# Row-tiled remainder matmuls, scores copied out as bf16, and rescaling on GpSimd in a fused attention forward and backward

## The chip, the core and the metric

The kernel runs on one core of one Trainium2 chip. The core has a matrix engine (TensorE, PE in the profile, with its weight loads as PEld), a vector engine (VectorE, DVE), an activation engine (ScalarE, ACT), a general engine (GpSimd, POOL), a queue that only issues DMAs (SyncE, SP), and 16 DMA engines. Matrix results land in PSUM; everything else lives in SBUF. The metric is the device time of one execution in microseconds (us), as the median of several runs.

## What is computed

The reference is one branchformer block and its backward pass, for x of shape 2 x 4000 x 144 in bf16. A layer norm feeds an attention branch and a gated convolution branch; both are merged by a depthwise convolution and a projection. What matters here is the attention:

```python
xa = _layernorm(x, axis=-1)
qkv = jnp.einsum('btd,de->bte', xa, w_qkv)
q, k, v = ...
scores = jnp.einsum('btd,bsd->bts', q, k) * D ** (-0.5)
p = _softmax(scores, axis=-1)
attn = jnp.einsum('bts,bsd->btd', p, v)
glob = jnp.einsum('btd,de->bte', attn, w_att_out)
...
_out, _vjp = jax.vjp(_f, x, w_qkv, w_att_out, ...)
_grads = _vjp(grad_out)
```

There are 4000 tokens and one head of width D = 144, so a row of scores has 4000 entries, and a contraction over D has 128 rows and a remainder of 16.

## The kernel before

**Tiling.** The two batches are worked on one after the other, by `phase_att` (L664) and then `Merge`. Inside `phase_att` a loop over t = 0 to 32 treats the 32 query tiles of 125 tokens (PB = 125). The 4000 keys are eight chunks c of 500 columns (CH = 500), taken two at a time as c2 = 0 to 3, so that a pair of chunks fills two PSUM banks: the tile `ps` of the pool `ps_sg`, which has two such buffers.

**One step t of the loop.** `S_pair(t, c2)` (L730) makes the scores of tile t. For each chunk there are two matmuls of 500 columns: L740 contracts the 128 main rows (`qt[:, 0]` against `xaTm`), L741 contracts the 16 remainder rows. The remainder of x lies in rows 96 to 111 of `R`, whose other rows hold something else, so the weights `qt[:, 1]` are zero outside those rows and the matmul runs over all 128 rows. VectorE then writes the negated scores into `Pbuf` and accumulates their minimum (L745, L747; this is the running negated row maximum `nm`), and ScalarE reads the same PSUM tile again and writes the exponential over it (L748). `rescale(t)` (L750) brings the first three pairs to the final maximum: `f` on ScalarE (L753), two multiplications on VectorE (L757) and one on ScalarE (L759). A DMA transpose on SP's queue then makes `PT` from `Pbuf` (L760).

Of the tile before, t - 1, `dP_pair` (L784) makes the gradient of the probabilities in the same way (L790, L791 with `qt[:, 2]`, `qt[:, 3]`), and one VectorE instruction (L794) subtracts `delta`, multiplies by `Pbuf` and writes `Sbuf`. `Y_half` (L762) multiplies `PT` by x, giving the attention output, the row sums, and `rl` and `delta`. A DMA transpose makes `ST` from `Sbuf` (L952), `Z_half` (L804) uses it one step later. `X_group` (L835) adds the gradient with respect to the keys, from `Sbuf`, `Pbuf` and the scaled queries `QBs` of two tiles, and VectorE adds it into `acc` (L855). `jit_mm` and `jit_tr` (L704, L717) prepare the weights `qt` of tile t + 1.

**Local units.** In between stand the units of the convolution branch (`local_units`, L419), one set for each two tiles: matmuls on PE, evacuations and tanh on ScalarE, some twenty small VectorE instructions and a few on GpSimd.

**What sets the order.** The code above is written as one stream. A scheduler then puts each engine's instructions into a fixed order, and each engine works through its own in that order, waiting where data is missing. PSUM pools hand out their buffers in turn: `ps_sg` has two (four banks), `ps_w` three, shared by everything else, and `ps_yz` one. `Pbuf` has four buffers, `Sbuf` three, `PT` and `ST` one each.

Of the kernel before, what the change touches and what calls it, by code (L numbers as in the profile page):

```python
# [336 lines left out]
def pre_pieces(k, W, b, S, pst):  # L337
# [4 lines left out]
    if True:  # L342
# [45 lines left out]
        def xat(g):  # L388
            pm = pst()
            for bi in range(8):  # L390
                nc.tensor.transpose(pm[:, bi, 0:PB], S.xa_aug[:, 8 * g + bi, 0:128], W.ident[0:PB, 0:PB])
            nc.scalar.copy(v8(S.xaT_m, 8 * g, 8), pm[:, :, 0:PB])
# [26 lines left out]
def local_units(k, W, b, S, A, es, DHT, ps_w):  # L419
# [52 lines left out]
    def e_h(g):  # L472
        nc.scalar.activation(q_[:], th[:], ACT.Copy, scale=0.5, bias=0.5)
# [24 lines left out]
    def e_gn(g):  # L498
        rs, t = rsr[slot(g)], gd(g + 1)
        nc.vector.scalar_tensor_tensor(rs[:, G2:2 * G2], live["mv"][:, :, 0], -1.0, rs[:, 0:G2], op0=ALU.mult, op1=ALU.mult)  # L500
        for bi in range(G2):
            nc.scalar.activation(t[:, 0, bi, :], hg[:, bi, D:2 * D], ACT.Identity, scale=rs[:, bi:bi + 1], bias=rs[:, G2 + bi:G2 + bi + 1])
# [12 lines left out]
    def e_m(g):  # L515
        nc.scalar.activation(th[:], q_[:], ACT.Copy, scale=-1.0, bias=1.0)
# [39 lines left out]
    def dgn_unit(g):  # L556
# [14 lines left out]
        for bi in range(G2):  # L571
            nc.scalar.activation(w_[:, bi, :], t[:, 0, bi, :], ACT.Identity, scale=nc1[:, bi:bi + 1], bias=c0[:, bi:bi + 1])
# [91 lines left out]
def phase_att(k, W, b, S, A, M, head=None):  # L664
# [6 lines left out]
    with ExitStack() as es:  # L671
# [16 lines left out]
        qrr = [ab.tile([PB, 2, 128], BF, name="qr%d" % i) for i in range(3)]  # L688
# [8 lines left out]
        xaTm, R, xaa = S.xaT_m, S.R, S.xa_aug  # L697
        QT, QB, RL, DL, YZ, ZN, ZT, NM, DHT = {}, {}, {}, {}, {}, {}, {}, {}, {}
        units, u0 = [], 0
# [4 lines left out]
        def jit_mm(i):  # L704
# [9 lines left out]
            nc.scalar.copy(qrr[i % 3][:, :, 96:112], pj[:].rearrange("p (a b) -> p a b", b=D)[:, :, 128:D])  # L714
            QB[i] = qb

        def jit_tr(i):  # L717
            qb = QB[i]
            pt = ps_w.tile([128, 4, 128], BF, tag="w")
            for h in range(2):  # L720
                for q, src in enumerate((qb[:, h, 0:128], qrr[i % 3][:, h, :])):
                    nc.tensor.transpose(pt[:, 2 * h + q, 0:PB], src, W.ident[0:PB, 0:PB])
# [7 lines left out]
        def S_pair(i, c2):  # L730
            qt = QT[i]
# [4 lines left out]
            ps = ps_sg.tile([PB, 2, 512], F32, tag="sg")  # L736
            for h in range(2):
                c = 2 * c2 + h
                cs = slice(c * CH, (c + 1) * CH)
                nc.tensor.matmul(ps[:, h, 0:CH], qt[:, 0, :], xaTm[:, cs], start=True, stop=False)  # L740
                nc.tensor.matmul(ps[:, h, 0:CH], qt[:, 1, :], R[:, cs], start=False, stop=True)  # L741
            src = ps[:, :, 0:CH].rearrange("p h (a b) -> p h a b", b=PB)
            pdst = pchunk(i % NPB, c2).rearrange("p (h a b) -> p h a b", h=2, b=128)[:, :, :, 0:PB]
            if c2 == 0:
                nc.vector.tensor_scalar(pdst, src, -1.0, None, op0=ALU.mult, op1=ALU.min, accum_out=nm[:, 0:1])  # L745
            else:
                nc.vector.tensor_scalar(pdst, src, -1.0, nm[:, c2 - 1:c2], op0=ALU.mult, op1=ALU.min, accum_out=nm[:, c2:c2 + 1])  # L747
            nc.scalar.activation(pdst, src, ACT.Exp, bias=nm[:, c2:c2 + 1], scale=1.0)  # L748

        def rescale(i):  # L750
# [3 lines left out]
            for c2 in range(3):  # L754
                pdst = pchunk(i % NPB, c2).rearrange("p (a b) -> p a b", b=128)[:, :, 0:PB]
                if c2 < 2:
                    nc.vector.tensor_scalar(pdst, pdst, f[:, c2:c2 + 1], None, op0=ALU.mult)  # L757
                else:
                    nc.scalar.activation(pdst, pdst, ACT.Copy, scale=f[:, c2:c2 + 1])  # L759
            nc.sync.dma_start_transpose(out=PT[:], in_=Pbuf[:, i % NPB, :])  # L760

        def Y_half(i, h):  # L762
            if h == 0:
# [12 lines left out]
            DL[i] = delta  # L776
            dj = small.tile([PB, D], BF, tag="dj", bufs=1)
            nc.vector.scalar_tensor_tensor(dj[:], Y[:, 0:D], rl[:], qb[:, 1, 0:D], op0=ALU.mult, op1=ALU.mult, accum_out=delta[:])
            yn = small.tile([PB, D], BF, tag="yn", bufs=2)
# [4 lines left out]
        def dP_pair(i, c2):  # L784
            qt = QT[i]
            ps = ps_sg.tile([PB, 2, 512], F32, tag="sg")
            for h in range(2):
                c = 2 * c2 + h
                cs = slice(c * CH, (c + 1) * CH)
                nc.tensor.matmul(ps[:, h, 0:CH], qt[:, 2, :], xaTm[:, cs], start=True, stop=False)  # L790
                nc.tensor.matmul(ps[:, h, 0:CH], qt[:, 3, :], R[:, cs], start=False, stop=True)  # L791
            psrc = pchunk(i % NPB, c2).rearrange("p (h a b) -> p h a b", h=2, b=128)[:, :, :, 0:PB]
            sdst = Sbuf[0:PB, i % NDB, c2 * 1024:(c2 + 1) * 1024].rearrange("p (h a b) -> p h a b", h=2, b=128)[:, :, :, 0:PB]
            nc.vector.scalar_tensor_tensor(sdst, ps[:, :, 0:CH].rearrange("p h (a b) -> p h a b", b=PB), DL[i][:], psrc, op0=ALU.subtract, op1=ALU.mult)  # L794

        def last_tr(c2):
# [5 lines left out]
            (nc.vector.tensor_copy if c2 % 2 else nc.scalar.copy)(PT[0:PB, 8 * c2:8 * c2 + 8, 0:PB], pt[0:PB, :, 0:PB])  # L802

        def Z_half(i, h, ST=ST):  # L804
# [785 lines left out]
```

## Time and profile before

| What | Value |
| --- | --- |
| Median of 3 runs | 1456.61 us (1455.83 to 1457.69) |
| The profiled execution | 1457.65 us, of which the span from first to last instruction is 1455.9 us |
| Granted TensorE clock | 0.99 of full speed |
| Steady stretch, 60.6 to 362.0 us: PE, DVE, ACT, POOL busy of 301.4 us | 293.54, 263.62, 195.44, 38.88 us |
| Start, 0 to 60.6 us: PE, DVE busy | 42.22, 42.02 us |
| Between the batches, 600 to 800 us: PE, DVE busy | 168.10, 136.51 us |
| End, 1340 to 1456 us: PE, DVE busy | 102.29, 65.09 us |

The busy time of an engine is the union of its instructions' spans. A matmul's recorded span is longer than the time until the next one can start, because matmuls are pipelined; the time that one costs PE is read from the distance of two starts. The loop over t takes most of the time: both batches together have 64 tiles, and all but the first two and the last steps look alike.

### The profile page before, as it was taken

The numbers are of one execution on the slowest core, as the hardware profiler recorded it, in microseconds if no ns is written. First come the engines' busy times: TensorE is split into PE (matmuls) and PEld (weight loads), VectorE is DVE, ScalarE is ACT, GpSimd is POOL, SyncE is SP. The second block draws the span as 40 slices with busy tenths as digits, with TensorE's granted clock in tenths as the row PEclk, the third lists the DMA queues.
The fourth block names the chain that finished last, engine by engine and source line by source line (L and its number), as shares of the span: only waits on it lengthen the run. The fifth ranks groups of instructions, "written<-read, shape, count | busy, mean of one in ns | idle before, by whom it ended". The sixth has DMA issues, their size and how long they took to land. (4 is left out here: it accounts for less than half of the span.)

```text
span 1455.9 us, 38963 instructions
## 1 busy us (share of the span) xinstructions
PE 1371.7 (94%) x16186; PEld 1180.2 (81%) x16186; DVE 1179.7 (81%) x2747; ACT 863.0 (59%) x1636; POOL 289.0 (20%) x515
## 2 busy tenths in 40 slices
PE   5999999999999999988887999999999999999898
PEld 3778888888888888887865888888888888888797
DVE  7799988888898988869457988888888888887754
ACT  6766666666666665525456666666666666554281
POOL 8411011111111110148212012111111111111420
PEclk9999999999999999999999999999999999999999
DMA  3586767666666666774236676666676666776712
GB/s 109 104 139 118 119 119 122 123 123 112 110 119 114 117 109 123 125 170 131 81 67 121 123 123 116 110 122 126 113 122 117 122 110 119 132 123 115 209 37 64
DMA packets 559391, 170.37 MB, mean 117 GB/s; under 512 B 542447, under 2 KB 554113, under 8 KB 559172
## 3 DMA queue, kind: packets, MB, share of 16 engines
q1 hardware_dynamic: 553578, 155.57, 58.0%
q0 software_dynamic: 5088, 12.11, 3.3%
q8 instruction: 126, 2.06, 0.6%
q14 instruction: 51, 0.42, 0.1%
q10 hardware_dynamic: 548, 0.21, 0.1%
HBM read 21.04 MB, written 14.12 MB: 24 GB/s over the span
## 5 line engine op out<-in xcount | busy, mean ns | idle before, releaser
L794 DVE SCALAR_TENSOR_TENSOR Sbuf<-ps,delta,Pbuf 125x1000 bf16<-125x1000 f32 x256 | 320.2, 1256 | 31.1 <-PE ps L791 29.0
L849 PE MATMUL X<-QBs,Sbuf 125*125 125x144 bf16 x2048 | 303.0, 226 | 6.5 <-DVE acc L855 2.7
L849 PE MATMUL X<-QBs,Pbuf 125*125 125x144 bf16 x2048 | 301.9, 226 | 0.0
L849 PEld LDWEIGHTS <-Pbuf 125*125 125x125 bf16 x2048 | 262.0, 137 | 15.2 <-issue 10.8
L849 PEld LDWEIGHTS <-Sbuf 125*125 125x125 bf16 x2048 | 261.9, 137 | 5.1
L855 DVE TENSOR_TENSOR acc<-X,acc 125x432 f32<-125x432 f32 x372 | 204.3, 552 | 36.5 <-PE X L849 35.7
L740 PE MATMUL ps<-xaT_m,qt 128*125 128x500 bf16 x512 | 193.2, 377 | 9.9 <-ACT Pbuf L748 6.7
L790 PE MATMUL ps<-xaT_m,qt 128*125 128x500 bf16 x512 | 191.8, 375 | 9.1 <-ACT Pbuf L748 6.1
L741 PE MATMUL ps<-R,qt 128*125 128x500 bf16 x512 | 192.3, 376 | 0.6 <-DVE R L357 0.4
L791 PE MATMUL ps<-R,qt 128*125 128x500 bf16 x512 | 191.0, 373 | 0.0
L768 PEld LDWEIGHTS <-PT 125*125 125x125 bf16 x2048 | 149.2, 138 | 28.2 <-DMA PT<-Pbuf 10.1
L768 PE MATMUL yz<-xa_aug,PT 125*125 125x145 bf16 x2048 | 152.4, 228 | 8.6 <-DMA PT<-Pbuf 8.5
L810 PEld LDWEIGHTS <-ST 125*125 125x125 bf16 x1984 | 143.8, 138 | 16.8
L810 PE MATMUL yz<-xa_aug,ST 125*125 125x144 bf16 x1984 | 147.7, 228 | 0.0
L745 DVE TENSOR_SCALAR_CACHE_REDUCE Pbuf<-ps 125x1000 bf16<-125x1000 f32 x64 | 76.7, 1198 | 23.7 <-PE ps L741 23.1
L595 POOL TENSOR_TENSOR A_dwc<-l_fl,A_dwc 128x512 f32<-128x512 f32 (+2 forms) x48 | 35.7, 743 | 295.9 <-ACT l_fl L594 295.9
L741 PEld LDWEIGHTS <-qt 128*125 128x125 bf16 x512 | 70.4, 137 | 28.7 <-issue 9.2
L791 PEld LDWEIGHTS <-qt 128*125 128x125 bf16 x512 | 69.6, 136 | 29.6 <-issue 9.3
L740 PEld LDWEIGHTS <-qt 128*125 128x125 bf16 x512 | 70.2, 137 | 22.2 <-issue 1.8
L790 PEld LDWEIGHTS <-qt 128*125 128x125 bf16 x512 | 69.7, 136 | 22.7 <-DVE Sbuf L794 2.1
L465 POOL TENSOR_SCALAR l_a<-l_sq 125x576 bf16<-125x576 bf16 x32 | 21.5, 671 | 299.5 <-ACT l_sq L463 260.2
L814 ACT ACTIVATE zn<-yz,rl 125x144 bf16<-125x144 f32 x64 | 24.1, 376 | 95.0 <-PE yz L810 94.9
(801 smaller groups left out, 3089.8 us busy)
## 6 DMA issues: line engine op xcount, KB each, us to landing
Yn_d<-yn SPq DMA_DIRECT2D x64, 35.2 KB
Zn_d<-zn SPq DMA_DIRECT2D x64, 35.2 KB
ug_d<-ugr SPq DMA_DIRECT2D x32, 70.3 KB
xo<-in_x_dram SPq DMA_DIRECT2D x16, 140.6 KB
out_dram<-dxo SPq DMA_DIRECT2D x16, 140.6 KB
go_h<-in_grad_out_dram POOLq DMA_DIRECT2D x4, 504.0 KB, 6.7
Zn<-Zn_d SPq DMA_DIRECT2D x4, 504.0 KB
PT<-Pbuf SPq DMA_TRANSPOSE x64
```

The lines of the kernel that those rows point to most:

```text
L595: nc.gpsimd.tensor_tensor(acc, fl[0:rows, 0:n], acc, op=ALU.add)
L740: nc.tensor.matmul(ps[:, h, 0:CH], qt[:, 0, :], xaTm[:, cs], start=True, stop=False)
L741: nc.tensor.matmul(ps[:, h, 0:CH], qt[:, 1, :], R[:, cs], start=False, stop=True)
L745: nc.vector.tensor_scalar(pdst, src, -1.0, None, op0=ALU.mult, op1=ALU.min, accum_out=nm[:, 0:1])
L768: nc.tensor.matmul(Y, PT[0:PB, j, 0:PB], xaa[:, j, 0:D + 1], start=(j == 0), stop=(j == NB - 1))
L790: nc.tensor.matmul(ps[:, h, 0:CH], qt[:, 2, :], xaTm[:, cs], start=True, stop=False)
L791: nc.tensor.matmul(ps[:, h, 0:CH], qt[:, 3, :], R[:, cs], start=False, stop=True)
L794: nc.vector.scalar_tensor_tensor(sdst, ps[:, :, 0:CH].rearrange("p h (a b) -> p h a b", b=PB), DL[i][:], psrc, op0=ALU.subtract, op1=ALU.mult)
L810: nc.tensor.matmul(Z, ST[0:PB, j, 0:PB], xaa[:, j, 0:D], start=(j == 0), stop=(j == NB - 1))
L814: nc.scalar.activation(zn[:, 0:D], Z, ACT.Copy, scale=RL.pop(i)[:])
L849: nc.tensor.matmul(X[:, jj, :], l, r, start=(n_ == 0), stop=(n_ == len(ops) - 1))
L855: nc.vector.tensor_tensor(av, X[:, 0:nj, :], av, op=ALU.add)
```

## The change

There are seven parts.

1. **Row positions.** A new tile `XR` holds the 16 remainder rows of x at partitions 0, 32, 64 and 96, chunk c at position c mod 4; SP's queue fills it with two DMAs behind each `xat` piece. The remainder weights are laid out by `rems` at the four positions too (two copies of 16 columns to each of two places, on GpSimd), and `jit_tr` transposes them. A remainder matmul now names 16 rows of one position.
2. **Groups of four.** `quad` makes two chunks of scores of tile t and two chunks of dP of tile t - 1: four main matmuls, then their four remainders at four different positions. It takes both `ps_sg` buffers. `products(q)` pairs score pair q with dP pair q^1. In the first step of a batch there is no dP (groups of two; in the first batch all at position 96), and in the second step of the first batch scores and dP still come in groups of two.
3. **Scores.** VectorE writes the negated scores as bf16 and the minimum of the pair alone; a VectorE instruction on one column joins it with the minimum so far; ScalarE takes the exponential from `Pbuf` in SBUF.
4. **dP.** Three of four pairs are copied from PSUM to `Sbuf` as bf16 by ScalarE and multiplied by `Pbuf` in SBUF by VectorE; the fourth is multiplied out of PSUM by VectorE as before. `delta` is no longer subtracted there: it enters through `ty` in Z (now on VectorE) and through the second half of `QBs`.
5. **GpSimd.** The rescaling of `Pbuf` (three multiplications, but for the first two tiles and the last), four instructions for `QBs`, and four steps of the local units that ScalarE had.
6. **Order in the step.** Z and Y halves, X groups and local units are placed at other points of the step; `ST` is transposed in two halves; the step t = 32 has two groups of four dP chunks.
7. **The end of a batch.** `last_tr` writes to `ST`, and Y of the last tile and `late_y` move behind it.

```diff
+            for c in (2 * g, 2 * g + 1):
+                nc.sync.dma_start(S.XR[32 * (c % 4):32 * (c % 4) + DR, (c // 4) * CH:(c // 4 + 1) * CH], S.R[96:112, c * CH:(c + 1) * CH])
...
-        nc.scalar.activation(q_[:], th[:], ACT.Copy, scale=0.5, bias=0.5)
+        nc.gpsimd.tensor_scalar(q_[:], th[:], 0.5, 0.5, op0=ALU.mult, op1=ALU.add)
...
-            nc.scalar.activation(w_[:, bi, :], t[:, 0, bi, :], ACT.Identity, scale=nc1[:, bi:bi + 1], bias=c0[:, bi:bi + 1])
+            nc.gpsimd.tensor_scalar(w_[:, bi, :], t[:, 0, bi, :], nc1[:, bi:bi + 1], c0[:, bi:bi + 1], op0=ALU.mult, op1=ALU.add)
...
-            nc.scalar.copy(qrr[i % 3][:, :, 96:112], pj[:].rearrange("p (a b) -> p a b", b=D)[:, :, 128:D])
+            for h in range(2):
+                rems(nc.gpsimd.tensor_copy, i, h)
...
+        def quad(work, stacked=True):
+            pp = [ps_sg.tile([PB, 2, 512], F32, tag="sg", name="ps") for _ in range(len(work) // 2)]
+            for r, (i, h, c) in enumerate(work):
+                mm = nc.tensor.matmul(pp[r // 2][:, r % 2, 0:CH], QT[i][:, 3 * h, :], xaTm[:, c * CH:(c + 1) * CH], start=True, stop=False)
+            with tc.issue_after(mm.ins), tc.high_priority():
+                for r, (i, h, c) in enumerate(work):
+                    q = c % 4 if stacked else 3
+                    rs = slice(32 * q, 32 * q + DR)
+                    xr = XR[rs, (c // 4) * CH:(c // 4 + 1) * CH] if stacked else R[rs, c * CH:(c + 1) * CH]
+                    nc.tensor.matmul(pp[r // 2][:, r % 2, 0:CH], QT[i][rs, 1 + (q // 2 + h) % 2, :], xr, start=False, stop=True)
...
-                nc.vector.tensor_scalar(pdst, src, -1.0, nm[:, c2 - 1:c2], op0=ALU.mult, op1=ALU.min, accum_out=nm[:, c2:c2 + 1])
-            nc.scalar.activation(pdst, src, ACT.Exp, bias=nm[:, c2:c2 + 1], scale=1.0)
+            nc.vector.tensor_scalar(pdst, src, -1.0, 3.0e38, op0=ALU.mult, op1=ALU.min, accum_out=nm[:, o:o + 1])
+            if c2:
+                nc.vector.tensor_tensor(nm[:, c2:c2 + 1], nm[:, c2 - 1:c2], nm[:, o:o + 1], op=ALU.min)
+            nc.scalar.activation(pdst, pdst, ACT.Exp, bias=nm[:, c2:c2 + 1], scale=-1.0)
...
+        def PdP(i, c2, src, direct):
+            if direct:
+                nc.vector.tensor_tensor(pv(Sbuf, i % NDB, c2), src, pv(Pbuf, i % NPB, c2), op=ALU.mult)
             else:
+                nc.scalar.copy(pv(Sbuf, i % NDB, c2), src)
+                sc = Sbuf[0:PB, i % NDB, c2 * 1024:(c2 + 1) * 1024]
+                nc.vector.tensor_tensor(sc, sc, pchunk(i % NPB, c2), op=ALU.mult)
...
+                if not quick:
+                    nc.gpsimd.tensor_scalar(p_, p_, f[:, c2:c2 + 1], None, op0=ALU.mult)
...
-            nc.scalar.activation(QBs[:, i % NPB], qb[:], ACT.Copy, scale=rl[:])
+            nc.gpsimd.tensor_scalar(QBs[:, i % NPB, 0, :], qb[:, 0, 0:D], rl[:], None, op0=ALU.mult)
+            nc.gpsimd.tensor_scalar(g1[:], qb[:, 1, 0:D], rl[:], None, op0=ALU.mult)
+            nc.gpsimd.tensor_scalar(g0[:], qb[:, 0, 0:D], nd[:], None, op0=ALU.mult)
+            nc.gpsimd.tensor_tensor(QBs[:, i % NPB, 1, :], g0[:], g1[:], op=ALU.add)
...
-            nc.scalar.activation(zn[:, 0:D], Z, ACT.Copy, scale=RL.pop(i)[:])
+            nc.vector.scalar_tensor_tensor(zn[:, 0:D], Z, RL.pop(i)[:], TY.pop(i)[:], op0=ALU.mult, op1=ALU.add)
...
+            def products(q):
+                ps = quad(S_work(t, q) + (dP_work(t - 1, q ^ 1) if ok(t - 1) else []))
+                S_exp(t, q, ps[0])
+                if ok(t - 1):
+                    PdP(t - 1, q ^ 1, ps[1], q == 3)
```

In each piece that follows, numbers behind a name tell buffers apart. On PE, in the middle of a batch, the end of a score pair before the change (`ps` the scores' PSUM tile, `qt` the weights, `PT` the transposed probabilities):

```order
L740 LDWEIGHTS qt_17119
L740 MATMUL ps_17363<-xaT_m_64,qt_17119 125x500
L741 LDWEIGHTS qt_17119
L741 MATMUL ps_17363<-R_65,qt_17119 125x500
L768 LDWEIGHTS PT_12340
L768 MATMUL yz_17328<-xa_aug1_10841,PT_12340 125x145
```

The same place after the change, from the last main matmul of a group on:

```order
L744 LDWEIGHTS qt_9017
L744 MATMUL ps_9761<-xaT_m_64,qt_9017 125x500
L750 LDWEIGHTS qt_9363
L750 MATMUL ps_9760<-XR_66,qt_9363 125x500
L750 LDWEIGHTS qt_9363
L750 MATMUL ps_9760<-XR_66,qt_9363 125x500
L750 LDWEIGHTS qt_9017
L750 MATMUL ps_9761<-XR_66,qt_9017 125x500
L750 LDWEIGHTS qt_9017
L750 MATMUL ps_9761<-XR_66,qt_9017 125x500
L804 LDWEIGHTS PT_119
L804 MATMUL yz_9609<-xa_aug0_75,PT_119 125x145
```

Before, each remainder stood behind its own main matmul; now the four remainders of two PSUM tiles, scores and dP, stand behind one another.

On DVE, at the turn from one tile to the next, before the change (L794 the dP product, L757 the rescaling, L855 an X group's addition, L579 a local unit):

```order
L794 SCALAR_TENSOR_TENSOR Sbuf_117<-ps_7943,delta_7928,Pbuf_116 125x8x125
L757 TENSOR_SCALAR Pbuf_116<-Pbuf_116,f_7935 125x8x125 x2
L855 TENSOR_TENSOR acc_68<-X_7956,acc_68 125x3x144
L579 TENSOR_TENSOR dhr0_983<-l_dd_993,gpr1_976 125x576
L794 SCALAR_TENSOR_TENSOR Sbuf_117<-ps_7975,delta_7928,Pbuf_116 125x8x125
```

And after it, for the first two groups of a step (L770 the scores out of PSUM, L782 the dP product in SBUF, L772 the joined minimum, L581 and L887 the local unit and the X addition):

```order
L770 TENSOR_SCALAR Pbuf_117,nm__8868<-ps_8858 125x8x125
L581 TENSOR_TENSOR dhr1_1020<-l_dd_1029,gpr2_1013 125x576
L782 TENSOR_TENSOR Sbuf_118<-Sbuf_118,Pbuf_117 125x1024
L770 TENSOR_SCALAR Pbuf_117,nm__8868<-ps_8923 125x8x125
L772 TENSOR_TENSOR nm__8868<-nm__8868 125x1
L887 TENSOR_TENSOR acc_69<-X_8909,acc_69 125x3x144
L782 TENSOR_TENSOR Sbuf_118<-Sbuf_118,Pbuf_117 125x1024
```

The rescaling has left this engine, and the scores of the second group now stand behind the product of the first, whose `Pbuf` is that of the tile just rescaled.

On POOL, the instructions of one step before the change (all of local units):

```order
L465 TENSOR_SCALAR l_a_987<-l_sq_986 125x576
L470 TENSOR_SCALAR l_a_987<-l_sq_986 125x576
L485 COPY ur2_969<-l_hg_991 125x288
L484 TENSOR_TENSOR rsr2_981<-ve_7139,mhalf_93 125x2
L507 COPY gd_rem_956<-gd2_950 125x2x32
```

And after it, where a step turns into the next (L822 to L826 make `QBs`, L791 rescales, L725 lays out the remainders, the rest are local units):

```order
L822 TENSOR_SCALAR QBs_121<-qb1_123,rl_7146 125x144
L824 TENSOR_SCALAR g1_7160<-qb1_123,rl_7146 125x144
L825 TENSOR_SCALAR g0_7159<-qb1_123,nd_7151 125x144
L826 TENSOR_TENSOR QBs_121<-g0_7159,g1_7160 125x144
L791 TENSOR_SCALAR Pbuf_117<-Pbuf_117,f_7190 125x1024 x3
L725 COPY qr1_126<-qb1_123 125x2x2x16
L725 COPY qr1_126<-qb1_123 125x4x16
L467 TENSOR_SCALAR l_a_1023<-l_sq_1022 125x576
L472 TENSOR_SCALAR l_a_1023<-l_sq_1022 125x576
L475 TENSOR_SCALAR l_q_1026<-l_th_1025 125x576
```

The rescaling stands behind the four instructions for `QBs`, which need the reciprocal row sums of the tile before, and ahead of the local units' next instructions.

More of the change, by code (lines that the diff above doesn't have):

```diff
@@ L948, in phase_att @@
[L948 to L952 removed]
+                    if s < 4:
+                        S_exp(t, s, quad(S_work(t, s), t > 0)[0])
+                    elif t:
+                        PdP(0, s - 4, quad(dP_work(0, s - 4))[0], s % 2 == 1)
+                for h in range(2 * t):
+                    st_half(h)
+                    Y_half(0, h)
```

200 lines of the change are left out of this document (105 added, 95 removed).

## The prediction

> **What bounds the kernel now.** I read the page's busy times first, then the stretches, then the timeline of one step, then the groups by shape.
>
> ```profile
> PE 1371.7 (94%) x16186; PEld 1180.2 (81%) x16186; DVE 1179.7 (81%) x2747; ACT 863.0 (59%) x1636; POOL 289.0 (20%) x515
> ...
> 60.60:362.00 301.40, 293.54 (x3361) 250.05 (x3360) 263.62 (x566) 195.44 (x370) 38.88 (x65) 1.00 0.68 120
> ...
> L748 ACT ACTIVATE Pbuf<-ps,nm__996 x1: 1096/1096/1096, 60.6 to 60.6; 125x1000 bf16<-125x1000 f32 x1
> ...
> L748 ACT ACTIVATE Pbuf<-ps,nm__5885 x1: 1097/1097/1097, 362.0 to 362.0; 125x1000 bf16<-125x1000 f32 x1
> ```
>
> PE is busiest. The second row (PE, PEld, DVE, ACT, POOL, granted clock, DMA share, GB/s) is a stretch of 16 whole steps of the loop: the score remainder L741 runs 128 times in it, eight times a step, and the exponentials L748 that open steps 2 and 18 start at its two ends (60.6 and 362.0). So a step takes 301.4/16 = 18.84 us, with DVE busy for 16.48, ACT for 12.2 and POOL for 2.4 of them.
>
> ```profile
> 401.33 0.38 PE L740 MATMUL ps<-xaT_m,qt 128*125 128x500 bf16 x1
> ...
> 401.54 0.37 PE L741 MATMUL ps<-R,qt 128*125 128x500 bf16 x1
> ...
> 401.75 0.38 PE L740 MATMUL ps<-xaT_m,qt 128*125 128x500 bf16 x1
> ...
> 401.97 0.37 PE L741 MATMUL ps<-R,qt 128*125 128x500 bf16 x1
> ...
> 402.18 0.28 PE L707 MATMUL pj<-RW,R 128*125 128x288 bf16 x1
> ...
> 402.38 1.26 DVE L747 TENSOR_SCALAR_CACHE_REDUCE Pbuf<-ps,nm__6525 125x1000 bf16<-125x1000 f32 x1 [0.33 <-PE ps L741]
> ...
> 402.74 0.22 PE L849 MATMUL X<-QBs,Pbuf 125*125 125x144 bf16 x1
> ...
> 402.80 0.22 PE L849 MATMUL X<-QBs,Sbuf 125*125 125x144 bf16 x1
> ```
>
> Columns: start, duration, engine, line. A matmul of 500 columns costs PE 0.21 us from start to start (401.33, 401.54, 401.75, 401.97, 402.18), main or remainder alike; one of 144 columns 0.06. With 210 matmuls a step (3361/16), 32 of them of 500 columns, that is 32 x 0.21 + 178 x 0.061 = 6.7 + 10.9 = 17.6 us of 18.84. **PE sets the pace**, with 1.2 us a step of waits. DVE, at 16.5, is not far behind, and the two wait for each other through PSUM.
>
> **The remainders.** A step spends 16 x 0.21 = 3.4 us on them, 0.84 for each four. After the change the four stand together, on 16 rows each at four positions. No row shows four at once, but some of the end's matmuls run on 16 rows already, between full ones:
>
> ```profile
> 1386.23 0.22 PE L1222 MATMUL fpt<-ident,goT 128*128 128x128 bf16 x1
> ...
> 1386.38 0.18 PE L1223 MATMUL fpt<-ident,goT 16*128 16x16 bf16 x1
> ...
> 1386.49 0.23 PE L1222 MATMUL fpt<-ident,goT 128*128 128x128 bf16 x1
> ```
>
> The 16-row matmul starts 0.15 us behind one whose 128 columns stream in 0.055 (at 0.21 for 500), and the next full one 0.11 behind its 16 columns: about 0.10 us is lost at each turn, 0.20 for a group. Bounds of a group: 0.20 + 0.21 = 0.41 if the four run wholly side by side; 0.20 + 4 x 0.21 = 1.04 if not at all. Between these, weight loads may stagger them by up to the 0.06 at which L849's weights follow each other: 0.41 + 3 x 0.06 = 0.59. I take 0.50, amid 0.41 and 0.59, since each of the four has rows, weights and PSUM bank of its own. The saving is 0.34 us for a group; there are 62 steps of four groups, so **248 x 0.34 = 84 us** (107 with 0.41, 62 with 0.59, a loss of 50 with 1.04). The first steps, in groups of two, lose about 1 us.
>
> The Trainium skill (TensorEngine Tiling (Array Packing), Key Properties) says that different tiles can load and multiply in parallel, and that changing the mode drains TensorE; the turns of 0.10 us agree with the second, and no row here shows the first. Its page TensorE: Matmul & The Clock Gate (Measured speedup vs the span model) gives 3.07 times for four row tiles of 512 columns: by that a group would take 0.84/3.07 + 0.20 = 0.47 us, an estimate from that page, and the sum would gain 92 instead of 84 us.
>
> **What DVE, ACT and POOL gain and lose.** Groups by shape (busy, mean ns):
>
> ```profile
> L794 DVE SCALAR_TENSOR_TENSOR Sbuf<-ps,delta,Pbuf 125x1000 bf16<-125x1000 f32 x256 | 320.2, 1256 | 31.1 <-PE ps L791 29.0
> L855 DVE TENSOR_TENSOR acc<-X,acc 125x432 f32<-125x432 f32 x310 | 185.8, 602 | 21.7 <-PE X L849 20.9
> L745 DVE TENSOR_SCALAR_CACHE_REDUCE Pbuf<-ps 125x1000 bf16<-125x1000 f32 x64 | 76.7, 1198 | 23.7 <-PE ps L741 23.1
> L759 ACT ACTIVATE Pbuf<-Pbuf,f 125x1000 bf16<-125x1000 bf16 x64 | 73.0, 1140 | 0.1
> L757 DVE TENSOR_SCALAR Pbuf<-Pbuf,f 125x1000 bf16<-125x1000 bf16 x128 | 57.1, 489 | 10.0 <-ACT f L753 9.9
> L516 ACT ACTIVATE l_th<-l_q 125x576 bf16<-125x576 bf16 x32 | 22.0, 689 | 0.5
> L578 DVE SCALAR_TENSOR_TENSOR l_dd<-pd,rsr,l_w 125x144 bf16<-125x144 f32 x64 | 21.6, 359 | 0.2 <-ACT l_w L572 0.2
> L468 DVE TENSOR_TENSOR l_z<-l_a,l_hs 125x576 bf16<-125x576 bf16 x32 | 14.6, 455 | 6.8 <-POOL l_a L465 6.8
> L554 DVE TENSOR_TENSOR l_dd<-dugr,l_gc 125x288 bf16<-125x288 bf16 x32 | 9.4, 294 | 0.0
> L392 ACT COPY xaT_m<-pt 128x1000 bf16<-128x1000 bf16 x8 | 7.9, 992 | 16.9 <-PE pt L391 16.9
> L568 DVE TENSOR_TENSOR nc<-s,rsr 125x2 f32<-125x2 f32 x32 | 5.2, 161 | 0.0
> ```
>
> DVE, a step: gone are four L794 (5.02 us) and two L757 (0.98). New are three bf16 products in SBUF of 1024 elements: L554 and L468 give 0.56 ns an element more, so 0.455 + 448 x 0.00056 = 0.71 each, 2.1; one product out of PSUM of 1000 elements, between L855 carried on at its 1.39 ns an element for all its span (1.39) and L794 (1.256), 1.25; three joined minima and one `nd` like L568, 0.64; Z's evacuation like L578, 0.36. The scores cost as in L745. Net -6.0 + 4.35: DVE goes from 16.5 to **14.8 us**.
>
> ACT: three copies of 1000 like L392 (3.0) and one more small one come, L759 and the local steps like L516 go; it stays near 12 of 18 and costs nothing, PE and DVE being the cover. The exponential now reads SBUF, where L759 takes 1.14 us for the same shape: nothing on the path.
>
> POOL's prices are its own shortest and longest of that form:
>
> ```profile
> L219 POOL TENSOR_SCALAR sWm<-raw,cols x10: 369/375/388, 13.5 to 22.7; 128x144 bf16<-128x144 bf16 x10
> ...
> L261 POOL TENSOR_SCALAR sr<-two,cols x20: 264/268/512, 33.1 to 38.3; 128x16 bf16<-128x16 bf16 x20
> ...
> L465 POOL TENSOR_SCALAR l_a<-l_sq x32: 667/671/674, 64.7 to 1243.7; 125x576 bf16<-125x576 bf16 x32
> ```
>
> (min/median/max ns.) From 16 to 144 elements it takes 0.107 us more, so 1024 take 0.375 + 880 x 0.00084 = 1.11; a tile's three rescalings 3.3 us. Four steps for `QBs` at 0.375 to 0.5 are 1.6, two `rems` 0.5, and the local steps that ACT gave up, two like L465 and four at about 0.5 for two tiles, 1.6. **POOL goes from 2.4 to 9.4 us**: room enough, but two things follow.
>
> **New waits.** First, the product of a step's first group needs chunk 1 rescaled. From the end of a tile's last group: 0.3 + 1.2 for the scores, 1.25 for the direct product standing between them and the minimum on DVE, 0.2, the exponential 1.1, `f` 0.3, two rescalings 2.2, and POOL's `QBs` partly ahead: 7 us. That group's own copy is ready about 6 us from there (Y, X groups, group, copy). DVE stands for some 1 us a step, with the next group's scores behind it. Second, POOL and DVE meet:
>
> ```profile
> 789.12 0.66 POOL L470 TENSOR_SCALAR l_a<-l_sq 125x576 bf16<-125x576 bf16 x1
> 789.22 0.88 DVE L474 TENSOR_TENSOR l_hg<-l_q,l_hs 125x576 bf16<-125x576 bf16 x1
> ...
> L474 DVE TENSOR_TENSOR l_hg<-l_q,l_hs x32: 439/457/877, 68.8 to 1246.8; 125x576 bf16<-125x576 bf16 x32
> ```
>
> A DVE instruction with both inputs in SBUF, begun while POOL worked, took 0.88 us instead of 0.457: it stood until POOL was done at 789.78. There are about 11.5 such a step (three products, 4.5 local ones, four tiny ones), and POOL is at work half of the time. At 0.2 us each (half of them meet it, with 0.4 left) DVE loses 2.3 us: 14.8 + 1.0 + 2.3 = 18.1 in the worst alignment; part of the two is the same wait, so about 17.5. The Trainium skill (SBUF — State Buffer, Who interferes with whom) states it as a rule, an exclusive lock on a shared port pair, and adds that outside two-port modes one SBUF input does not contend; the pair of rows agrees. Price of this term: nothing, if DVE stays below PE's pace, up to the second rival's.
>
> Third, a group takes both `ps_sg` buffers, so the next cannot start until the last is out of PSUM. In the timeline DVE starts on the scores 0.41 us behind the last matmul's start (401.97, 402.38) and takes 1.2: 1.6 us, 1.4 beyond that matmul's own. On PE's side, by the new order, some 20 narrow matmuls (1.2 us) stand between a step's first two groups and mostly 30 or more behind the others. So 0.2 us is open at one gap, more where DVE is late: **0.35 us a step, 62 x 0.35 = 22 us**, from 0 to 1.0 us a step.
>
> SP: a transpose holds its queue for 4.82 us, and `PT` is now asked for some 4 us later:
>
> ```profile
> 411.61 4.82 SPq L760 DMA_TRANSPOSE PT<-Pbuf  x1
> ```
>
> Issued 8 us behind a tile's last group and landing by 13 to 14, it is needed at about 17.5. The half transposes of `ST` stand ahead of or behind it without delay. `XR`'s small DMAs lie in the start's load time. Cover gone, the price is the lateness itself, per step. The end of a batch has the same work in another order: 0, between -5 and +5 us.
>
> **Sum.** -84 + 22 + 1 = -61 us: a step of 18.84 - 1.36 + 0.35 = 17.8 us, against DVE's 17.5. On the profiled execution (1457.65 us, 1455.9 of span and 1.75 around it) that gives 1396.6; it stands 1.04 above the median of the runs, so **1395 us**.
>
> **The rivals.**
> - *Full overlap, no new waits* (0.41 us a group, DVE's waits all in its slack): 107 us less, 1350. For it: PE's waits are short now, and DVE loses work. Against it: DVE with its waits is as long as PE's step.
> - *DVE becomes the pace*: 14.8 + 1.0 + 2.3 and 0.3 of its waits for PE make 18.4 us a step, 0.45 less than now: 1429. For it: the 0.88 us row and POOL's 9.4 us.
> - *Slower, by the same lock*: 18.84 - 14.8 = 4.0 us a step is the point from which DVE's waits decide against the change, 0.35 us for each of the 11.5. If each meets a whole POOL instruction (about 0.45 us in the mean) it is 5.2, a step of 20.0: 62 x 1.15 = 71 more, 1528. Against it: the row shows a wait for what is left, not for the whole.
> - *The four do not run side by side*, so that the change doesn't do what it says: +50 + 22, 1529.
>
> **How the numbers follow.** Forecast 45%, held between 1370 and 1415; full overlap 21%, 1335 to 1370; DVE's pace 18%, 1415 to 1452; the lock 11%; no overlap 5%. The range leaves out the last two: 1335 to 1452. About 0.2% (3 us) is what a measurement can tell from no change: faster 0.80, same 0.05, slower 0.15.
>
> **What would show it.** Four L750 starting within 0.2 us, and 0.10 us lost on each side, show the group right; starts 0.21 apart show it wrong. L794's 320 us give way to some 140 us of L782 and 80 of L778. L782 far above 0.71 us in the mean, or DVE's idle time ahead of it put down to POOL, shows the lock and the first wait; PE's idle time ahead of L744, put down to DVE or ACT, shows the third. A PE idle ahead of Y on `PT`, which I put at nothing, would make the prediction wrong, as would a step above 18.4 us.

## The result, and the profile after

The changed kernel takes **1835.91 us** in the median of 4 runs (1834.07 to 1839.20), against 1456.55 us: a ratio of 1.2606 (1.2584 to 1.2628). The forecast was 1395 us, with a range from 1335 to 1452. It was wrong in sign and by 441 us.

The page of the changed kernel gives the span and the busy times (us, share of the span, instructions):

```profile
span 1837.4 us, 40065 instructions
...
PE 1454.2 (79%) x16190; PEld 1186.6 (65%) x16190; DVE 1132.6 (62%) x2947; ACT 851.8 (46%) x1451; POOL 1104.5 (60%) x1267
```

DVE has lost work as forecast, but no engine is near its limit any more, and POOL has gone from 289.0 to 1104.5 us. The view by core adds the mean granted clock of TensorE, of the kernel before and of the changed one:

```profile
core 0: 1455.9 us, clock 0.990
```

```profile
core 0: 1837.4 us, clock 0.880
```

PE's busy time times its clock is about its work at full clock: 1358 us before and 1280 after, 78 less. The rest of the busy time was lost to the clock (14 us before, 174 after), and what is left of the span is idle (84 and 383). So the 381.5 us come from **PE's work -78, clock +161, idle +299**. The mean clock is that of the whole span, idle time included; added up over stretches of 1 us, the work comes to 1361 and 1286 us, so the three parts hold to a few us. The same 16 steps as in the prediction, between the exponentials that open steps 2 and 18 (PE, PEld, DVE, ACT, POOL, clock):

```profile
71.60:465.90 394.30, 312.14 (x3368) 252.73 (x3368) 250.19 (x614) 188.37 (x317) 257.17 (x280) 0.87 0.51 91
```

A step takes 24.6 us instead of 18.84; POOL is busy for 16.1 us of it, where the prediction had 9.4. The groups by shape (busy, mean ns, idle time of the engine ahead and who ended it) show where:

```profile
L791 POOL TENSOR_SCALAR Pbuf<-Pbuf,f 125x1024 bf16<-125x1024 bf16 x180 | 515.1, 2873 | 5.0 <-ACT f L787 4.8
...
L770 DVE TENSOR_SCALAR_CACHE_REDUCE Pbuf<-ps 125x1000 bf16<-125x1000 f32 x256 | 306.0, 1195 | 70.6 <-PE ps L750 70.3
...
L778 DVE TENSOR_TENSOR Sbuf<-ps,Pbuf 125x1000 bf16<-125x1000 f32 x67 | 80.2, 1197 | 0.5 <-PE ps L750 0.3
```

A rescaling costs 2.87 us, not the 1.11 of the prediction. The view of one line gives its spread (min/median/max ns):

```profile
L791 POOL TENSOR_SCALAR Pbuf<-Pbuf,f x180: 2834/2845/3412, 94.4 to 1700.1; 125x1024 bf16<-125x1024 bf16 x180
```

Even the fastest of the 180 takes 2.83 us, so this isn't an instruction that is usually quick and sometimes held up by a neighbour: every one is slow. The waits say who stood for it (us in total, times, the longest):

```profile
DVE Sbuf L782 <- POOL Pbuf L791: 273.7, 57, 7.1
...
PE ps L744 <- DVE Pbuf L770: 131.6, 69, 6.5
```

The timeline shows how one wait becomes the other, in one step:

```profile
440.82 8.49 POOL L791 TENSOR_SCALAR Pbuf<-Pbuf,f 125x1024 bf16<-125x1024 bf16 x3
...
446.52 1.60 DVE L782 TENSOR_TENSOR Sbuf<-Sbuf,Pbuf 125x1024 bf16<-125x1024 bf16 x1 [5.04 <-POOL Pbuf L791]
...
449.80 0.81 DVE L580 SCALAR_TENSOR_TENSOR l_dd<-pd,rsr,l_w 125x144 bf16<-125x144 f32 x2 [1.25 <-POOL l_w L574]
...
450.52 1.19 DVE L770 TENSOR_SCALAR_CACHE_REDUCE Pbuf<-ps 125x1000 bf16<-125x1000 f32 x1
...
451.77 0.99 PE L744 MATMUL ps<-xaT_m,qt 128*125 128x500 bf16 x2 [4.74 <-DVE Pbuf L770]
```

The first product of the step stands 5.04 us for the second of three rescalings (and takes 1.60 us beside the third, where the median of L782 is 0.693). The next scores, L770, are queued behind it on DVE, and so are steps of a local unit, which stand 1.25 us more for `l_w`, queued behind the rescaling on POOL. The scores hold a PSUM tile that the second half of PE's next group needs, and PE stands for 4.74 us. What follows is in the stretches of 2 us (PE's busy time behind the length, the granted clock third from the end):

```profile
446.00:448.00 2.00, 1.03 (x12) 0.72 (x11) 1.48 (x1) 0.00 (x0) 2.00 (x2) 1.00 0.00 0
448.00:450.00 2.00, 0.00 (x0) 0.00 (x0) 0.75 (x6) 0.00 (x0) 2.00 (x3) 1.00 0.00 0
450.00:452.00 2.00, 0.23 (x1) 0.18 (x1) 1.92 (x5) 0.00 (x0) 0.56 (x3) 0.78 0.82 155
452.00:454.00 2.00, 2.00 (x13) 0.88 (x12) 2.00 (x7) 1.29 (x2) 0.00 (x0) 0.50 1.16 217
...
456.00:458.00 2.00, 2.00 (x13) 1.60 (x12) 0.51 (x1) 2.00 (x4) 0.00 (x0) 0.51 1.13 212
458.00:460.00 2.00, 2.00 (x24) 1.40 (x23) 1.07 (x1) 1.50 (x5) 0.00 (x0) 1.00 0.10 22
```

The clock falls to half at about 451 us and stays there until 458, some 7 us. PE works through 6.2 of them, from 451.77 on, and loses half of that, 3.1 us, on top of the 4.7 us of the wait. The Trainium skill (TensorE: Matmul & The Clock Gate, Part 1: The HAM clock gate) states this as a rule, half rate after an idle window of about 3.4 us until a busy one has passed; these rows agree in the rate, 0.50, and the kernel before, whose PE hardly ever stood so long, ran at 0.990.

One thing went as forecast. The remainders of a group:

```profile
458.16 0.38 PE L744 MATMUL ps<-xaT_m,qt 128*125 128x500 bf16 x1
458.46 0.43 PE L750 MATMUL ps<-XR,qt 16*125 16x500 bf16 x4
...
458.82 0.34 PE L462 MATMUL ph<-Wi,xaT_m 128*125 128x288 bf16 x1
```

All four start within 0.01 us (each lasts 0.42, the four 0.43). The last main matmul has streamed its 500 columns by 458.16 + 0.21 = 458.37, the next full one starts at 458.82: **0.45 us for a group**, where the prediction took 0.50.

### The profile page after: what moved, and what is told of

Read it like the earlier page. It is cut to its first block, busy times and chain, and to the rows that moved or that the text cites. A ratio compares the mean times of both kernels' runs of the same rounds, so it can differ in the third digit from the quotient of the medians.

```text
span 1837.4 us, 40065 instructions
## 1 busy us (share of the span) xinstructions
PE 1454.2 (79%) x16190; PEld 1186.6 (65%) x16190; DVE 1132.6 (62%) x2947; ACT 851.8 (46%) x1451; POOL 1104.5 (60%) x1267
## 5 line engine op out<-in xcount | busy, mean ns | idle before, releaser
L791 POOL TENSOR_SCALAR Pbuf<-Pbuf,f 125x1024 bf16<-125x1024 bf16 x180 | 515.1, 2873 | 5.0 <-ACT f L787 4.8
L744 PE MATMUL ps<-xaT_m,qt 128*125 128x500 bf16 x1024 | 304.8, 414 | 145.6 <-DVE Pbuf L770 131.6
L782 DVE TENSOR_TENSOR Sbuf<-Sbuf,Pbuf 125x1024 bf16<-125x1024 bf16 x189 | 179.4, 949 | 291.5 <-POOL Pbuf L791 273.7
L770 DVE TENSOR_SCALAR_CACHE_REDUCE Pbuf<-ps 125x1000 bf16<-125x1000 f32 x256 | 306.0, 1195 | 70.6 <-PE ps L750 70.3
L744 PEld LDWEIGHTS <-qt 128*125 128x125 bf16 x1024 | 138.5, 149 | 197.1 <-issue 165.8
L887 DVE TENSOR_TENSOR acc<-X,acc 125x432 f32<-125x432 f32 x372 | 203.0, 551 | 69.7 <-PE X L881 68.0
L780 ACT CAST Sbuf<-ps 125x1000 bf16<-125x1000 f32 x189 | 188.4, 997 | 72.8 <-PE ps L750 71.9
L804 PE MATMUL yz<-xa_aug,PT 125*125 125x145 bf16 x2048 | 153.7, 236 | 25.1 <-DMA PT<-Pbuf 25.1
L804 PEld LDWEIGHTS <-PT 125*125 125x125 bf16 x2048 | 143.8, 144 | 39.3 <-DMA PT<-Pbuf 28.1
L822 POOL TENSOR_SCALAR QBs<-qb,rl 125x144 bf16<-125x144 bf16 x64 | 41.7, 651 | 202.9 <-DVE rl L810 202.5
L750 PE MATMUL ps<-XR,qt 16*125 16x500 bf16 x1016 | 122.3, 459 | 0.0
L778 DVE TENSOR_TENSOR Sbuf<-ps,Pbuf 125x1000 bf16<-125x1000 f32 x67 | 80.2, 1197 | 0.5 <-PE ps L750 0.3
L574 POOL TENSOR_SCALAR l_w<-gd,nc,c 125x144 f32<-125x144 bf16 x64 | 29.9, 473 | 64.8 <-DVE nc L570 64.0
L1208 PE MATMUL po<-VUl,YT 128*125 128x144 bf16 x640 | 54.0, 231 | 7.0 <-ACT goT L350 7.0
```

The source lines that it names most:

```text
L744: mm = nc.tensor.matmul(pp[r // 2][:, r % 2, 0:CH], QT[i][:, 3 * h, :], xaTm[:, c * CH:(c + 1) * CH], start=True, stop=False)
L750: nc.tensor.matmul(pp[r // 2][:, r % 2, 0:CH], QT[i][rs, 1 + (q // 2 + h) % 2, :], xr, start=False, stop=True)
L770: nc.vector.tensor_scalar(pdst, src, -1.0, 3.0e38, op0=ALU.mult, op1=ALU.min, accum_out=nm[:, o:o + 1])
L778: nc.vector.tensor_tensor(pv(Sbuf, i % NDB, c2), src, pv(Pbuf, i % NPB, c2), op=ALU.mult)
L780: nc.scalar.copy(pv(Sbuf, i % NDB, c2), src)
L782: nc.vector.tensor_tensor(sc, sc, pchunk(i % NPB, c2), op=ALU.mult)
```

## The experiments

The first question was why L791 costs 2.85 us. The rows that gave the prediction its price, L219 and L261, multiply by a column and then by 1.0; L791 multiplies once. Run 1 gives L791 the second multiplication, run 2 the three steps for `QBs` as well:

```diff
-nc.gpsimd.tensor_scalar(p_, p_, f[:, c2:c2 + 1], None, op0=ALU.mult)
+nc.gpsimd.tensor_scalar(p_, p_, f[:, c2:c2 + 1], 1.0, op0=ALU.mult, op1=ALU.mult)
```

> In the changed kernel each of the 180 rescalings L791 on POOL took 2.84 us (the fastest 2.83), where the prediction had worked out 1.11 from L219 and L261. Those two rows multiply twice (by the column, then by 1.0); L791 multiplies once. This run gives L791 the second multiplication by 1.0 and changes nothing else. Theory A, the instruction's form sets the price: L791 falls to 1.1 us (0.9 to 1.3), a step's three rescalings from 8.5 to 3.3 us, DVE's idle time ahead of L782 put down to L791 from 274 us to under 70, and the time comes to 1380 to 1430 us, near the prediction's 1395. Rival B, POOL is slow here for the length, the writing in place, the 125 partitions or DVE beside it: L791 stays at 2.8 us and the time at 1836 us.

> As the run before, and the three POOL steps for QBs (L822, L824, L825: 125x144, one multiplication, 0.65 us each) get the second multiplication too. Theory A: each falls from 0.65 to 0.38 to 0.47 us, POOL loses 0.6 us more a step, and the time is that of the run before or up to 10 us less, since only the rescaling behind them on POOL waits for them. Rival B: 0.65 us as before, no change to the run before.

Run 1 took 1544.19 us, a ratio of 1.0588 (1.0560 to 1.0616). Its line L791, and L822 of run 2:

```profile
L791 POOL TENSOR_SCALAR Pbuf<-Pbuf,f x180: 1107/1118/1649, 93.2 to 1406.6; 125x1024 bf16<-125x1024 bf16 x180
```

```profile
L822 POOL TENSOR_SCALAR QBs<-qb,rl x64: 371/379/680, 70.0 to 1424.3; 125x144 bf16<-125x144 bf16 x64
```

One more multiplication makes the instruction 2.5 times faster: 2.845 to 1.118 us, and 0.645 to 0.379 for L822. Theory A holds for the price and rival B falls. The time fell by 292 us, three quarters of the loss, and stayed above the 1380 to 1430 expected: something else costs some 90 us. Run 2 took 1524.28 us (1.0446, 1.0411 to 1.0481), 20 less, where at most 10 were expected. DVE's wait for L791, 273.7 us in the changed kernel, is 95.8 us in run 1 (under 70 was expected), and in run 2:

```profile
DVE Sbuf L782 <- POOL Pbuf L791: 62.8, 49, 3.5
```

Run 12 asks the same away from the rescaling, in the kernel before (L219 here, L261 likewise):

```diff
-                nc.gpsimd.tensor_scalar(t[:, ch, kk, :], self.Wm[h][:, ch, :], col, 1.0, op0=ALU.mult, op1=ALU.mult)
+                nc.gpsimd.tensor_scalar(t[:, ch, kk, :], self.Wm[h][:, ch, :], col, None, op0=ALU.mult)
```

> The kernel before, with the second multiplication by 1.0 taken away from L219 (ten of 128x144) and L261 (twenty of 128x16), both written to another tile, on 128 partitions, in the start. It asks for the price of the form by itself, away from the rescaling. Theory A: L219 goes from 0.375 to 0.65 us and L261 from 0.268 by about 0.03 at most, for a slope of 2.5 ns an element; L296 (128x128), left with two operations, stays at 0.37. Rival B (writing in place, 125 partitions or the length): both stay as they were.

```profile
L219 POOL TENSOR_SCALAR sWm<-raw,cols x10: 629/634/652, 13.0 to 23.8; 128x144 bf16<-128x144 bf16 x10
...
L261 POOL TENSOR_SCALAR sr<-two,cols x20: 316/318/763, 32.9 to 38.8; 128x16 bf16<-128x16 bf16 x20
...
L296 POOL TENSOR_SCALAR dgm<-ident,cols x5: 367/367/379, 47.2 to 48.6; 128x128 bf16<-128x128 bf16 x5
```

L219 goes from 0.375 to 0.634 us and L261 from 0.268 to 0.318, while L296, left as it was, stays. Neither place, partitions, length nor writing in place matter: it is the form. The slope is (634 - 318) / 128 = 2.47 ns an element with one multiplication and 0.84 with two. The time, 1456.98 us in one run, doesn't notice these thirty.

Runs 3 and 4 ask what the remaining loss has to do with the rescaling. Run 3 takes it off POOL. Run 4 is run 2 with another order: the first product of a step takes the pair that needs no rescaling.

```diff
-                rescale(t, t == NB - 1)
+                rescale(t, True)
```

```diff
-                ps = quad(S_work(t, q) + (dP_work(t - 1, q ^ 1) if ok(t - 1) else []))
+                ps = quad(S_work(t, q) + (dP_work(t - 1, 3 - q) if ok(t - 1) else []))
...
-            for c2 in range(3):
+            for c2 in (2, 1, 0):
```

> The rescaling goes back to two multiplications on DVE and one on ACT in every step (the branch that the first and last steps use already); all else as in the changed kernel, L822 to L825 with one multiplication. If the rescaling on POOL is the whole cause (theory A as well as rival B): no wait of that length is left, the step is 17.5 to 18.8 us, the time 1380 to 1460. Rival C, the groups of four themselves (both ps_sg buffers at once, remainders behind a priority) or POOL's lock against DVE hold the kernel up: it stays above 1600 us, with PE idle ahead of L744.

> As the second run (all POOL steps with two multiplications), and a step's products take the chunk pairs in the order 3, 2, 1, 0 instead of 1, 0, 3, 2, with the rescaling in the order 2, 1, 0 and the two half transposes of ST exchanged: the first product then needs the pair that is not rescaled at all. If the first product's wait for the rescaling still sets the step after theory A's repair (1.0 us a step by the prediction), DVE's idle time ahead of L782 put down to L791 goes to under 10 us and the time falls by up to 62 us against the second run. If PE or the lock sets the step, it is within 5 us of the second run.

Run 3 took 1520.48 us (1.0425, 1.0396 to 1.0454). It fits neither range: the long wait is gone, the time is that of run 2, and 64 us are still lost. The two differ in the form of the three steps for `QBs` as well, so they don't compare POOL with DVE and ACT cleanly; runs 4 and 8 do. Run 4 took 1512.10 us (1.0387, 1.0347 to 1.0428). DVE no longer stands for L791 (62.8 us of it in run 2), and the time fell by 12 us, a fifth of the 62 that the first expectation allowed: the first product's wait was part of the loss, and mostly something else took its place.

Run 5 is run 4 with the slow form in L791 alone, to separate the price from the place where it is waited for; run 8 is run 4 with the rescaling off POOL.

> The fourth run (order 3, 2, 1, 0) with the rescaling L791 back to its one multiplication (2.84 us each, 8.5 a step). It separates the price from the place where it is waited for. Place (the first product's wait, with the scores queued behind it on DVE, makes the loss): the first product needs no rescaled pair, the later ones have 2.8 us per pair between groups some 5 us apart, so DVE's idle time ahead of L782 put down to L791 falls from 274 us to under 60 and the time is 1510 to 1580, most of the 292 us that the second multiplication gained. Price (POOL, at 16 us a step, and PT behind 8.5 us of rescaling set the step wherever it is waited for): 1700 or more, with PE idle ahead of Y on PT.

> The fourth run, with the rescaling on DVE and ACT in every step. In the fourth run L782 takes 0.83 us in the mean and 0.69 in the median: by the prediction's lock it stands for POOL. If that lock costs what the prediction said (2.3 us a step less what remains without the rescaling), the time falls by 20 us or more; if it is small, the 1.0 us a step that DVE takes on makes up for it: within 10 us of the fourth run's 1512, either side.

Run 5 took 1777.39 us (1.2187, 1.2112 to 1.2261). By the time, place falls and price holds: the wait for L791 is gone, and of the 379 us lost only 59 are won back. The path is a wider one than either expectation named. PE does stand ahead of Y for `PT`, 54.9 us against 20.6 in run 4, but DVE's waits for POOL are longer:

```profile
DVE l_z L470 <- POOL l_a L467: 77.8, 23, 7.4
DVE l_dd L580 <- POOL l_w L574: 76.0, 20, 7.0
DVE rsr L502 <- POOL rsr L486: 54.9, 24, 7.3
```

With 8.5 us of rescaling in POOL's queue, whatever DVE needs from POOL comes late: the first product no longer stands, and the local branch does, for 209 us in these three lines, against 49 in run 4. Run 8 took 1522.67 us (1.0445, 1.0406 to 1.0484), 11 above run 4, near the second expectation. The products in run 4 and in run 8:

```profile
L782 DVE TENSOR_TENSOR Sbuf<-Sbuf,Pbuf 125x1024 bf16<-125x1024 bf16 x189 | 157.5, 833 | 22.3 <-ACT Sbuf L780 21.9
```

```profile
L782 DVE TENSOR_TENSOR Sbuf<-Sbuf,Pbuf 125x1024 bf16<-125x1024 bf16 x189 | 132.4, 701 | 20.6 <-ACT Sbuf L780 19.0
```

L782 falls from 0.833 to 0.701 us in the mean: POOL's lock against DVE is there, and worth 0.4 us a step in the three products (0.13 each). What comes back to DVE costs more: two multiplications a step, and 23.1 us in all of standing for `f` ahead of them.

Run 6 is run 4 with the four local steps back on ACT (L475 here; L504, L518 and L574 likewise), run 7 is run 4 with the remainders one behind the other:

```diff
-        nc.gpsimd.tensor_scalar(q_[:], th[:], 0.5, 0.5, op0=ALU.mult, op1=ALU.add)
+        nc.scalar.activation(q_[:], th[:], ACT.Copy, scale=0.5, bias=0.5)
```

```diff
-        def quad(work, stacked=True):
+        def quad(work, stacked=False):
```

> The fourth run, with the four local steps (L475, L504, L518, L574) back on ACT, as in the kernel before. What is open: the fourth run is still 56 us behind the kernel before, and in 16 of its steps DVE stands 20 us for POOL's results of the local branch, with the scores queued behind. Theory D, these longer local chains hold DVE and through it PE: the time falls by 15 to 40 us, to 1470 to 1497, and DVE's idle times put down to L475 and L574 (34 us) go. Rival E, the groups' claim on both PSUM buffers holds PE: within 5 us of the fourth run's 1512, the idle time only moves to other lines.

> The fourth run, with all remainders at row position 96, so that the four of a group cannot run side by side; same order, same PSUM buffers. By the prediction's bounds a group's remainders go from 0.50 to 1.04 us: PE's busy time rises by up to 248 x 0.54 = 134 us. If PE sets the pace in the fourth run, the time is 1600 to 1650; if its idle time (1.9 us a step) absorbs a part, 1540 to 1600; if the four never ran side by side, within 5 us of 1512.

Run 6 took 1493.09 us (1.0250, 1.0211 to 1.0288), 19 less, as theory D expected: the local steps on POOL cost time. It is the fastest version of the change found here, and still slower than the kernel before. Run 7 took 1569.32 us (1.0763, 1.0726 to 1.0799), 57 more than run 4, within the middle range. Its page and a group of it:

```profile
PE 1472.1 (94%) x16190; PEld 1155.4 (74%) x16190; DVE 1127.4 (72%) x2947; ACT 848.3 (54%) x1451; POOL 763.4 (49%) x1267
```

```profile
458.64 1.06 PE L750 MATMUL ps<-R,qt 16*125 16x500 bf16 x4
459.63 0.28 PE L854 MATMUL pt<-ident,zn 125*128 125x125 bf16 x2
```

At one position the four take 1.06 us, against 0.43 at four. At full clock PE's work is 1472.1 x 0.967 = 1424 us, 135 more than in run 4 (1328.4 x 0.970 = 1289); the prediction's bounds gave 134. Only 57 of them reach the time, since PE stands for 177 us in run 4 and for 97 here.

Runs 9 to 11 followed what run 6 still loses. Its span is 31.6 us longer than before. Measured between the first exponentials of the tiles, 10.4 of it lie ahead of step 2 of batch 0 (71.0 against 60.6 us), 4.1 between the batches, 12.5 behind those of the last tile, and 4.6 in all the steps between. The end, in run 6 (SP's queue, whose rows show how long a transpose held it, then PE):

```profile
1364.48 21.08 SPq L796 DMA_TRANSPOSE PT<-Pbuf  x1
...
1389.92 0.38 PE L804 MATMUL yz<-xa_aug,PT 125*125 125x145 bf16 x1 [11.85 <-DMA PT<-Pbuf]
```

In the changed kernel itself PE stood there too:

```profile
1740.11 0.38 PE L804 MATMUL yz<-xa_aug,PT 125*125 125x145 bf16 x1 [14.67 <-DMA PT<-Pbuf]
```

Runs 9 to 11 are each built on the one before. Run 9 is run 6 with another opener for the big loads of `go_h`; run 10 also moves `Y` of tile 0 in step 1; run 11 also puts one more X group between a step's first two groups.

```diff
-                M.open_early(ST)
+                M.open_early(PT)
```

```diff
+                    if t and s in (2, 3):
+                        Y_half(0, s - 2)
                 for h in range(2 * t):
                     st_half(h)
-                    Y_half(0, h)
```

```diff
             loc(0.5)
-            x(1)
+            x(2)
             products(1)
```

> The sixth run (order 3, 2, 1, 0, two multiplications, local steps on ACT), with one word changed: the copy that opens the big loads of go_h at a batch's end waits for PT instead of ST. What is open: in the sixth run the last PT transpose of batch 1 takes 21.1 us instead of 4.8, and PE stands 11.9 us for it (4.2 in batch 0); PT is now issued behind the ST half that opens the loads, in the kernel before it was issued ahead. If the loads hold the transpose up: PT takes about 5 us again, PE's idle time ahead of L804 goes from 16 us to under 3, and the time falls by 8 to 16 us, to 1477 to 1485. If PT was late for another reason: within 4 us of 1493.

> As the run before, and in step 1 of batch 0 the two halves of Y of tile 0 stand behind the third and fourth group, as in the kernel before, instead of at the step's end. What is open: from the first exponentials of step 1 to those of step 2 it is 30 us in all versions of the changed kernel, and 18.9 in the kernel before. If the place of Y, ahead of step 2's first group, makes it: that stretch falls by 4 to 8 us, and the time with it. If the two-matmul groups and their queues in the first steps make it, nothing changes (within 3 us).

> As the run before, and two of a step's X groups instead of one stand between its first and second group of four, so that PE has 12 more narrow matmuls (0.75 us) there. If the claim on both PSUM buffers at that gap still costs what the sixth run shows ahead of L744 (0.3 us a step), the time falls by 5 to 18 us; if DVE's queue sets the step, the wait moves elsewhere and the time stays within 5 us.

In run 9 the loads were indeed what held the transpose up:

```profile
1375.60 5.67 SPq L796 DMA_TRANSPOSE PT<-Pbuf  x1
```

PE's idle time ahead of L804, put down to `PT`, fell from 19.4 to 3.7 us, but the time was 1497.02 us (1.0282, 1.0255 to 1.0309), no less than run 6: the intervals of the two overlap. The loads now come later, and between the batches PE stands for what they bring, a wait that run 6 didn't have:

```profile
PE Hps L1129 <- POOL go_r L1096: 5.9, 1, 5.9
```

Run 10 (1502.28 us; 1.0302, 1.0275 to 1.0328) and run 11 (1508.74 us; 1.0351, 1.0323 to 1.0379) gained nothing: moving `Y` or an X group there didn't win back what is lost. In run 10 the stretch from step 1 to step 2 stays at 30 us.

PE's side of these runs, worked out as above (us; work is busy time times clock):

| Run | span | PE work | lost to the clock | PE idle |
| --- | --- | --- | --- | --- |
| before | 1455.9 | 1358 | 14 | 84 |
| changed | 1837.4 | 1280 | 174 | 383 |
| 1, L791 with two multiplications | 1542.1 | 1290 | 51 | 201 |
| 4, and QBs, order 3, 2, 1, 0 | 1505.0 | 1289 | 40 | 177 |
| 5, as 4, slow L791 | 1772.4 | 1282 | 138 | 352 |
| 6, as 4, local steps on ACT | 1487.5 | 1278 | 45 | 164 |
| 7, as 4, one row position | 1568.9 | 1424 | 49 | 97 |

What the clock takes grows with the idle time, though not by it alone: run 7 loses 49 us beside 97 idle, run 4 loses 40 beside 177.

## Why the prediction was wrong

**The step that failed** is the sentence "From 16 to 144 elements it takes 0.107 us more, so 1024 take 0.375 + 880 x 0.00084 = 1.11; a tile's three rescalings 3.3 us." Its rows were for another form of the instruction. A row names operation, engine and shape; that L219 and L261 do two operations and the new line one stands only in the code. The trace of before held no POOL multiplication by a column with a single operation. It was an operation that the trace doesn't show, and it got no bounds, where the others had them. Measured: 2.845 us, 8.5 a step. For the form of its rows the working was right: 1.118 us in run 1 against 1.11.

**The path of the loss in the changed kernel was the prediction's own first wait,** which the sum put at nothing as long as DVE stays below PE's pace. It had the chain of the first product at 7 us against 6, one us a step. With two rescalings of 2.845 instead of 1.11 the chain is 3.5 us longer: 4.5 us a step, 270 for the 60 steps with POOL's rescaling. DVE stood 273.7 us. With it the prediction's own 14.8 us of DVE's work become 19.3 a step, above the 17.8 of PE, so the wait couldn't be hidden any more. At the right price, in run 2, it stood 62.8 us, about the one us a step that was worked out. The slower rival named the lock instead and gave it 1528 us; the lock was over-priced (2.3 us a step). In run 4 DVE is busy for 248.84 us in 16 steps, 15.6 a step against the 14.8 that were worked out without any lock, so it costs at most 0.8 by that sum.

**No term for the clock.** A wait was priced at its own length. In the changed kernel PE's waits cost about half as much again through the clock: 161 us beside 299 of idle time.

**"Room enough" on POOL was judged by its busy time alone.** At the right price that time is 10.6 us a step (run 2), near the 9.4 of the prediction. But run 5 shows that the queue counts: DVE takes results of every local unit from POOL, and they stand behind 8.5 us of rescaling, so that the wrong price costs most of the loss even where the first product doesn't wait for it.

**What held.** The remainders: 0.45 us for a group against 0.50, all four at once, 135 us of PE work between one position and four against 134. PE's work fell by 78 us, against 84 less the 1 us of the first steps. The products: L778 1.197 us against 1.25, L782 0.693 in the median against 0.71. The third wait, 22 us: in run 6, with the other waits gone, PE stands ahead of L744 for

```profile
PE ps L744 <- DVE Pbuf L770: 20.9, 38, 1.5
```

**What was too small beside it.** The first steps were put at 1 us and cost 10.4 in run 6. The end was put at 0, with 5 either way, and costs 12.5 in run 6, in part since half of `ST` opens the loads about when `PT` is asked for (run 9 got 5.0 back there, and paid 10.7 between the batches). The wait ahead of Y on `PT`, put at nothing, is 25.1 us in the changed kernel, 14.7 of them at this place. The prediction looked for what stands ahead of PT's transpose on SP's queue, not for what the half transposes set free. The local steps on POOL were counted in its busy time alone, and cost 19 us. Run 6, without the faults that were found, is 35 us above the kernel before, where the sum had -61.

**What stays open.** In run 6 PE still stands for 164 us, 80 more than before, though its work fell by 80. Most of it lies in the steps themselves: between the exponentials that open steps 2 and 31 of both batches PE is busy for 1024 us against 1084 before, and idle for 93 against 29, so that what the remainders save is lost again as waits, of which the third wait is a fifth. The waits in its steps are short and spread over many lines (20.9 us ahead of L744, 14.9 for DVE's sums L887, 10.5 for `ST`, 10.0 for `QBs`); runs 10 and 11 didn't find one place that makes them. Why the first steps lose 10 us wasn't found either; PE isn't waiting there so much as busy for longer, 50.5 us against 42.2. Whether a single operation with a constant in place of a column is slow too wasn't tried.

## What to carry to other kernels

Before a duration is taken from a row, compare the code of both instructions: the same operation and shape in the profile can be two forms with a factor of 2.5 between them. An operation that the trace doesn't show in exactly its form gets bounds, and the first thing to ask of it is at which price the plan fails; here the plan broke at a wait whose length grew with twice that price. And a wait of TensorE isn't priced by its length alone: behind 4.7 us of it the clock stood at half for some 7 us.

## What the hardware showed that was not expected

On POOL, `tensor_scalar` by a column with one operation takes 2.47 to 2.5 ns an element (125x1024: 2.845 us; 128x144: 0.634), with a second multiplication by 1.0 it takes 0.84 (1.118; 0.375). The Trainium skill (GPSIMD Engine Reference, Elementwise — side-by-side cycle accounting) gives 1.03 cycles an element for its shortest loop bodies (k up to 2), 0.86 ns by its clock of 1.2 GHz, an estimate from that page. The form with two operations agrees with it; the one with a single operation, the simpler of the two, needs about three times as much.

A DMA transpose that mostly holds SP's queue for 4.8 us held it for 21.08 us in run 6, while the loads of `go_h` ran, and for 5.67 in run 9, where they were opened behind it. The row of the queue doesn't tell when the data is there: in the changed kernel it shows 7.31 us from 1716.32, and PE's first matmul on `PT` started at 1740.11:

```profile
1716.32 7.31 SPq L796 DMA_TRANSPOSE PT<-Pbuf  x1
```
